# Attention and mixture of experts on one core: two output tiles and one memory tile for the attention's results, scatters to disjoint views, the 64-row block second

## The chip, the cores and the metric

The kernel runs on one core of one Trainium2 chip. The time is the device time of one execution in microseconds. The kernel before took 972.42 us (median of three runs, 971.52 to 975.38). The engines are named as in the profile: PE multiplies matrices, DVE and ACT are the vector and the scalar engine, POOL is the general one, SP issues transfers. PSUM is the memory that PE writes, in eight banks of 128 x 512 float32.

## The reference

For 8 batches and 8 heads, with 576 rows of 64 columns, the kernel computes a causal softmax attention and a retrieval from a memory, mixes both by a gate per head, and sends the 4608 rows of 512 through a mixture of 8 experts, each of which takes exactly 576 rows, chosen greedily from the largest logit down.

```python
scores = np.where(causal, -1e9, scale * q @ k.T)
a = exp(scores - max); a /= a.sum(-1) + 1e-09
local = a @ v
q_p = phi(q)                       # x+1 if x > 0, else exp(x)
mem_out = (q_p @ M_prev) / (q_p @ z_prev + 1e-06)
x = g * mem_out + (1 - g) * local  # 4608 x 512
logits = x @ w_gate                # 4608 x 8
for idx in np.argsort(-logits.flatten()):
    tok, e = idx // E, idx % E     # taken if tok is free and e has room (576)
out[mask_e] = np.maximum(x[mask_e] @ w1[e], 0.0) @ w2[e]
```

## The kernel before

*Attention.* The work is cut into 16 units, one batch and four heads each. For a unit, q, k and v are loaded, split into two float16 parts each, and transposed by PE. For a head, PE computes the scores into the buffers `pb`; DVE takes the row maxima (L1197); ACT takes exponentials to float16 (`ph`, L1334), and the rest that float16 leaves out goes to `pl`: ACT writes the exponential again in float32, in PSUM (L1338) or in SBUF (L1341), and then DVE (L1339, called P2v) or POOL (L1342, called P2) subtracts `ph`. A string `p2k` of twelve letters says for each block of a unit which of the two it is.

`outs` (L1351) makes a head's result. The memory part AVm takes ten matmuls (`avs<-mh,pT`), the attention part AV1, AV2 and AV3 45 matmuls of 65 columns. All go into one PSUM tile `avs` of three banks. There are two head buffers in it: buffer b has slots 0 to 6 in bank 2b and slots 7 to 9 in a part of the middle bank 1. Slots 0 to 4 take the attention, 5 to 9 the memory, and column 64 of a slot has the denominator. Then DVE works: N0 (L1385 and L1386) takes the ten denominators, N1 (L1390) inverts them, N2 (L1389, `xt<-avs`) scales the memory part into `xt`, N2b (L1389, `avs<-avs`) scales the attention part in place, and N3 (L1403) adds the two. In one head of four, N2 scales all ten slots and POOL adds (L1397). After that come a cast, a subtraction, transposes and the logits of the rows.

*Order.* A list scheduler, run when the kernel is built, puts all instructions in one order from costs given with each node (`SC.add('AVm',[('T',300)],...)`: 300 ns on PE), from limited buffers (`av`=2 head buffers) and from two tables of numbers, PR for the attention and PM for the experts: due times, offsets and biases that choose an engine where several can do a node. An engine runs its instructions in that order. The waits between engines are put in by the tile framework from the tiles that instructions read and write.

*Routing and experts* (`moe_all`, L1537). For each expert a threshold is found in 12 rounds (DVE L1774, ACT L1772, PE, DVE L1780 and L1781). The 576 rows that pass are listed: DVE counts (L1612) and computes row numbers `idx` (L1614), and POOL fetches the rows by five indirect transfers (L1617). Weights come as float32 and are split into `wh` and `wl` by ACT (L1688, L1689) and POOL (L1690); for the first pieces of expert 0 by ACT (L1685) and DVE (L1686). PE multiplies by the first matrix (`ph`, `prem`), ACT and DVE take the relu in two parts (L1732, L1733), PE multiplies by the second (`py`) in row blocks of 128, 128, 128, 128 and 64. A block of 128 is copied by ACT to `ys` (L1747); the block of 64 is put together by ACT (L1749) and DVE (L1750). POOL writes each block to its rows by an indirect transfer (L1752), and `chain('scat')` makes each of the 40 wait for the one before. Routing of expert n+1 runs beside the matmuls of expert n.

Of the kernel before, what the change touches and what calls it, by code (L numbers as in the profile page):

```python
# [23 lines left out]
          'kba': -30628.42,  # L24
          'kbd': -21514.39,
          'kbv': -30457.33,
          'kha': -9689.05,
          'khp': 68039.52,
          'khv': 14252.18,
          'klp': -32138.21,  # L30
          'klv': -19015.13,
          'mh2a': 18046.34,
          'mh2v': -7557.72,
          'mha': -6556.62,
          'mhv': 118047.29,
          'mlp': -61301.72,
          'mlv': 103205.55,
          'mra': 13094.26,
          'mrv': -49929.19,
          'mza': 13667.92,  # L40
          'mzv': 154718.09,
          'nap': -923.34,
          'nav': -3267.9,
          'nca': -17356.34,
          'ncp': 19952.5,
          'ncv': -19147.84,
          'nsp': -33806.3,
          'nsv': 8700.47,
          'p2p': 3448.83,
          'p2v': -5.41,  # L50
          'p4sp': -99613.75,
          'p4sv': -14317.61,
          'pha': -24715.3,
          'php': 10489.25,
          'phra': -10695.76,
          'phrv': 20287.52,
          'phv': -24278.1,
          'plp': 4297.99,
          'plv': 4879.76,
          'prepca': -46562.05,  # L60
          'prepcv': -134550.89,
          'qha': -51241.95,
          'qhp': 17974.64,
          'qhv': -60171.16,
          'qlp': 26287.18,
          'qlv': 78420.0,
          'qmovea': 42586.74,
          'qmoved': 5914.55,
          'qmovev': -9885.0,
          'tea': -3123.88,  # L70
          'tev': -3783.25,
          'vha': -3050.15,
          'vhp': 15722.78,
          'vhv': 48350.7,
          'vlp': 27996.84,
          'vlv': 29979.61,
          'xtea': -62406.89,
          'xtev': 142184.48},
 'dl': {'0': {'AV': 3.03,
              'MX': -439.58,  # L80
              'N': -45.87,
              'P2': 95.25,
              'S': -79.48,
              'fin1': 396.93,
              'fin2': 87.35,
              'kb': 3.48,
              'kh': -937.23,
              'kl': -795.9,
              'kt': 387.88,
              'lk': -688.72,  # L90
              'lm': -210.42,
              'lq': -541.06,
              'lv': -99.14,
              'maxrem': -157.75,
              'mfin': 328.48,
              'mfin2': -56.76,
              'mfin3': -180.29,
              'mh': -838.83,
              'ml': 193.21,
              'mz': -1034.64,  # L100
              'nadd': -286.28,
              'ncast': 852.81,
              'nsub': -703.35,
              'ph': -141.8,
              'phe': -764.62,
              'phr': -38.36,
              'phs': 62.7,
              'pl': -977.2,
              'prep': 200.37,
              'proc24': 671.37,  # L110
              'pt': 192.37,
              'qh': -404.47,
              'ql': 386.07,
              'qmove': 129.64,
              'qt': -168.61,
              'sj4': -1434.02,
              'vh': 667.29,
              'vl': 490.09},
        '1': {'AV': 58.78,
              'MX': -104.28,  # L120
              'N': -347.1,
              'P2': -339.06,
              'S': 606.52,
              'fin1': 484.59,
              'fin2': 2.45,
              'kb': 126.23,
              'kh': -563.06,
              'kl': 507.8,
              'kt': 591.73,
              'lk': -540.92,  # L130
              'lm': -577.58,
              'lq': -166.76,
              'lv': -66.59,
              'maxrem': 342.62,
              'mfin': -545.34,
              'mfin2': 9.06,
              'mfin3': -80.01,
              'mh': -618.46,
              'ml': 449.29,
              'mz': 14.48,  # L140
              'nadd': -926.32,
              'ncast': -198.57,
              'nsub': 506.43,
              'ph': -560.71,
              'phe': -372.41,
              'phr': -876.37,
              'phs': 209.62,
              'pl': 213.14,
              'prep': 164.36,
              'proc24': 454.72,  # L150
              'pt': 233.41,
              'qh': -427.92,
              'ql': 1274.93,
              'qmove': 1075.02,
              'qt': 47.11,
              'sj4': -45.54,
              'vh': -285.68,
              'vl': -176.11},
        '10': {'AV': 758.58,
               'MX': -73.66,  # L160
               'N': 72.38,
               'P2': 279.63,
               'S': -8.46,
               'fin1': -248.92,
               'fin2': 347.06,
               'kb': 358.91,
               'kh': 442.41,
               'kl': 79.29,
               'kt': -298.24,
               'lk': -767.97,  # L170
               'lm': 14.63,
               'lq': -633.6,
               'lv': 673.6,
               'maxrem': 724.62,
               'mfin': -318.66,
               'mfin2': 386.87,
               'mfin3': 137.35,
               'mh': 981.75,
               'ml': -129.7,
               'mz': 550.95,  # L180
               'nadd': -120.05,
               'ncast': 1.51,
               'nsub': -229.44,
               'ph': 489.25,
               'phe': 997.89,
               'phr': -1284.21,
               'phs': 165.79,
               'pl': -224.45,
               'prep': 191.53,
               'proc24': -144.35,  # L190
               'pt': -242.79,
               'qh': 501.96,
               'ql': 984.38,
               'qmove': -284.76,
               'qt': -711.9,
               'sj4': -187.91,
               'vh': 1156.16,
               'vl': -17.9},
        '11': {'AV': 355.99,
               'MX': -108.14,  # L200
               'N': -177.3,
               'P2': -1118.12,
               'S': 356.14,
               'fin1': 358.76,
               'fin2': 223.29,
               'kb': -146.64,
               'kh': -152.48,
               'kl': 559.23,
               'kt': -15.25,
               'lk': 955.17,  # L210
               'lm': 246.97,
               'lq': 882.81,
               'lv': -420.65,
               'maxrem': 30.53,
               'mfin': -41.22,
               'mfin2': 83.89,
               'mfin3': -400.44,
               'mh': -51.28,
               'ml': -126.76,
               'mz': -129.3,  # L220
               'nadd': 107.08,
               'ncast': -1366.45,
               'nsub': 536.08,
               'ph': -283.95,
               'phe': -649.23,
               'phr': -270.74,
               'phs': -481.4,
               'pl': 292.58,
               'prep': -518.41,
               'proc24': -4.05,  # L230
               'pt': -249.01,
               'qh': 480.34,
               'ql': 615.5,
               'qmove': 459.89,
               'qt': -26.77,
               'sj4': 164.57,
               'vh': -414.34,
               'vl': 21.65},
        '12': {'AV': 167.39,
               'MX': 1.03,  # L240
               'N': 559.11,
               'P2': -154.37,
               'S': -49.69,
               'fin1': 221.57,
               'fin2': 527.79,
               'kb': 1200.71,
               'kh': -74.53,
               'kl': -144.63,
               'kt': -309.14,
               'lk': -221.84,  # L250
               'lm': -263.39,
               'lq': -614.17,
               'lv': 244.4,
               'maxrem': 565.59,
               'mfin': 257.23,
               'mfin2': 16.16,
               'mfin3': 507.27,
               'mh': 215.36,
               'ml': 291.75,
               'mz': 463.51,  # L260
               'nadd': -356.78,
               'ncast': 12.76,
               'nsub': 868.62,
# [631 lines left out]
class Sched:  # L895
# [18 lines left out]
    def run(self,tol=100,sem=170,same=110,t0=0.0,hwg=450,dlat=1300,dend=950,ph=2800.0,thr=3060,pel=60):  # L914
# [20 lines left out]
        def pick(e):  # L935
            C=cand[e]; best=None; L=[]; Q=line[e]
            f=free[e]
            for c in C:
# [7 lines left out]
                elif e=='V' and (x.slack or x.nm in LK) and s<poolb-1: s=poolb-1  # L946
# [11 lines left out]
        while left:  # L958
            b=None
# [931 lines left out]
```

## Time and profile before

| | |
|---|---|
| median of three runs | 972.42 us (971.52 to 975.38) |
| profiled execution | 974.23 us, span 972.40 us |
| PE, PEld busy | 814.7 us (84%), 523.4 us |
| DVE, ACT, POOL busy | 717.4 us (74%), 578.3 us, 599.7 us (62%) |
| attention | 0 to about 500 us |
| first expert's threshold and list | about 500 to 560 us |
| experts' matmuls | about 560 to 962.5 us |
| mean granted clock of PE | 0.947 |

The span is from the first to the last instruction of the profiled execution; its time as a run is 1.83 us longer. Busy shares of the whole span are means over these stages. A wait in the profile is idle time of an engine, put down to the instruction whose end came last; the chain of waits is followed back from the last instruction.

### The profile page before, as it was taken

Reading aid. Unit: us, or ns where it says so; the run is one execution under the profiler, and the core shown is the slowest. Engines: PE = TensorE matmul, PEld = TensorE weight load, DVE = VectorE, ACT = ScalarE, POOL = GpSimd, SP = SyncE. Lnnn points to the kernel's source line nnn. Section 1 sums busy time; section 2 is a strip of 40 time slices with the busy share of each in tenths; the row PEclk is TensorE's granted clock in tenths of the full one; section 3 lists DMA queues with packets and bytes.
Section 4 is the critical chain, followed back from the end, with each engine's and each line's share of the span. In section 5 each row is a group of like instructions: output and inputs, shape, how many; then the busy total and the mean of one; then the engine's idle time right before and its main releaser. Section 6 shows DMA issues by size and latency. Waiting matters only on the chain.

```text
span 972.4 us, 25309 instructions
## 1 busy us (share of the span) xinstructions
PE 814.7 (84%) x9736; PEld 523.4 (54%) x9736; DVE 717.4 (74%) x2385; ACT 578.3 (59%) x1046; POOL 599.7 (62%) x594
## 2 busy tenths in 40 slices
PE   4587888878888888888831797999999999999995
PEld 3365666656667666767620543445454444444442
DVE  8998889998889899896678977768787777502010
ACT  4475776677587767768622557483838383754110
POOL 7768787889889878968610237382647373585101
PEclk9897999999899999999955699899999999999999
DMA  5566454528555443533411427362737273692101
GB/s 130 117 142 147 111 118 93 128 66 168 115 131 124 92 105 69 118 66 66 94 36 61 162 79 220 127 177 81 231 102 237 94 232 102 216 269 78 38 12 38
DMA packets 230302, 116.49 MB, mean 120 GB/s; under 512 B 199013, under 2 KB 208229, under 8 KB 230181
## 3 DMA queue, kind: packets, MB, share of 16 engines
q1 hardware_dynamic: 224293, 96.00, 39.1%
q0 software_dynamic: 5888, 18.88, 5.8%
q8 instruction: 76, 1.25, 0.5%
q14 instruction: 45, 0.37, 0.1%
HBM read 72.40 MB, written 18.87 MB: 94 GB/s over the span
## 4 chain that ended last, share of the span: by engine, by line
PE 44%; DVE 7%; issue 1%; ACT 1%; DMA 1%; POOL 0%; POOLq 0%; DVEq 0%; ACTq 0%
PE py L1540 19%; PE ph L1540 16%; PE avs L1041 3%; PE prem L1540 2%; DVE scr L1774 2%; PE pr L1540 1%; DMA out_dram<-ys,idx 1%; PE pb L1041 1%; DVE xt L1389 1%; PE pl L1540 1%; DVE avs L1389 1%; DVE xt L1403 0%; DVE th L1781 0%; ACT wh L1689 0%; DVE kk L1780 0%
## 5 line engine op out<-in xcount | busy, mean ns | idle before, releaser
L1690 POOL TENSOR_TENSOR wl<-wst,wh 128x1024 f16<-128x1024 f32 x60 | 127.6, 2150 | 81.9 <-ACT wh L1689 64.7
L1540 PE MATMUL ph<-xT,wh 128*128 128x512 f16 (+1 forms) x560 | 164.0, 368 | 1.7 <-DVE hl L1733 1.0
L1334 ACT ACTIVATE ph<-pb 128x512 f16<-128x512 f32 x192 | 115.7, 602 | 42.5 <-PE pb L1041 32.0
L1197 DVE TENSOR_REDUCE mx<-pb 128x1 f32<-128x512 f32 (+3 forms) x256 | 123.3, 547 | 2.2 <-PE pb L1041 2.0
L1041 PE MATMUL avs<-V,ph 128*128 128x65 f16 x1792 | 103.6, 194 | 24.8 <-DVE xt L1389 11.4
L1752 POOL DMA_INDIRECT out_dram<-ys,idx x40 | 38.7, 968 | 126.3 <-ACT ys L1747 70.9
L1041 PEld LDWEIGHTS <-ph 128*128 128x128 f16 x1792 | 94.3, 99 | 33.4 <-issue 30.3
L1342 POOL TENSOR_TENSOR pl<-pf,ph 128x512 f16<-128x512 f32 x80 | 95.2, 1193 | 19.7 <-ACT pf L1341 18.3
L1041 PE MATMUL pb<-qT,kT 128*128 128x64 f16 (+3 forms) x576 | 102.3, 242 | 6.0 <-DVE mx L1197 2.8
L1540 PEld LDWEIGHTS <-wh 128*128 128x128 f16 x1072 | 68.7, 99 | 59.3 <-issue 3.8
L1041 PE MATMUL avs<-V,pl 128*128 128x65 f16 x896 | 99.5, 197 | 0.0
L1540 PE MATMUL ph<-xT,wl 128*128 128x512 f16 (+1 forms) x280 | 98.8, 367 | 0.0
L1041 PE MATMUL pb<-kT,qM 128*128 128x256 f16 (+5 forms) x384 | 83.9, 314 | 16.9 <-DVE mx L1197 9.4
L1041 PE MATMUL pb<-qM,kB 128*128 128x64 f16 (+3 forms) x576 | 97.1, 241 | 0.1
L1540 PE MATMUL py<-wl,hh 128*128 128x512 f16 x256 | 97.0, 379 | 0.0
L1540 PE MATMUL py<-wh,hh 128*128 128x512 f16 x256 | 97.0, 379 | 0.0
L1540 PE MATMUL prem<-xT,wh 128*128 128x64 f16 x512 | 96.7, 193 | 0.0
L1733 DVE SCALAR_TENSOR_TENSOR hl<-ph,hh 128x512 f16<-128x512 f32 x64 | 44.0, 688 | 65.2 <-ACT hh L1732 64.6
L1774 DVE TENSOR_SCALAR_CACHE_REDUCE scr<-p_LwT,th 128x320 f16<-128x320 f32 x168 | 85.1, 544 | 2.7
L1772 ACT ACTIVATE scs<-p_LwT,th 128x320 f16<-128x320 f32 x84 | 47.0, 560 | 64.8 <-DVE th L1781 50.7
L1041 PEld LDWEIGHTS <-pl 128*128 128x128 f16 x896 | 85.2, 99 | 0.0
L1732 ACT ACTIVATE hh<-ph 128x512 f16<-128x512 f32 x64 | 37.9, 594 | 74.9 <-PE ph L1540 49.6
(289 smaller groups left out, 2293.1 us busy)
## 6 DMA issues: line engine op xcount, KB each, us to landing
wst<-in_moe_w_dram SPq DMA_DIRECT2D x32, 1024.0 KB
kf<-in_k_dram SPq DMA_DIRECT2D x64, 128.0 KB
qf<-in_q_dram SPq DMA_DIRECT2D x64, 128.0 KB
vf<-in_v_dram SPq DMA_DIRECT2D x64, 128.0 KB
xd<-xs SPq DMA_DIRECT2D x16, 512.0 KB
kB<-kT SPq DMA_DIRECT2D x15, 288.0 KB
kf<-in_k_dram SPq DMA_DIRECT2D x32, 32.0 KB
qf<-in_q_dram SPq DMA_DIRECT2D x32, 32.0 KB
```

The costliest lines, as they stand in the source:

```text
L1041: def MM(*a,**kw): mm(*a,skip_group_check=True,**kw)
L1197: R=lambda o,i: nc.vector.tensor_reduce(o,i,axis=mybir.AxisListType.X,op=ALU.max)
L1334: c=SC.add('Eh',[('A',478)],lambda x,a=a: nc.scalar.activation(phs_[x.buf['ph']][:,0:512],pbb[a.buf['pb']],AF.Exp,scale=0.125),acq=('ph',) ...
L1342: e=SC.add('P2',[('P',1113)],lambda x,c=c,d=d: nc.gpsimd.tensor_sub(pls_[c.buf['ph']][:,0:512],pfs[d.buf['pf']],phs_[c.buf['ph']][:,0:512] ...
L1389: MU=lambda o,i,d: nc.vector.tensor_tensor(o,i,d,op=ALU.mult)
L1540: def MM(*a,**kw): mm(*a,skip_group_check=True,**kw)
L1690: SC.add('sp',[('P',2079)],lambda x,ws=ws,k=k,s=s: G_.tensor_sub(wl[:,k,s],ws(),wh[:,k,s]),r=[key+('h',)],w=[key+('l',)],after=[b],rel=rel ...
L1732: b=SC.add('hh',[('A',478)],lambda x,a0=a0,f=f: A_.activation(hh[:,f],phb[a0.buf['ph']],AF.Relu),w=[('hh',f)],after=[y],prio=pr('hh',n,pos ...
L1733: SC.add('hl',[('V',602)],lambda x,a0=a0,f=f: V_.scalar_tensor_tensor(hl[:,f],phb[a0.buf['ph']],0.0,hh[:,f],op0=ALU.max,op1=ALU.subtract), ...
L1752: z=SC.add('scat',[('P',655 if i<4 else 330,'p',0,(1034,'n'))],lambda x,e=e,i=i,r_=r_: G_.indirect_dma_start(out=out,out_offset=bass.Indir ...
L1772: SC.add('sign',[('A',547)],lambda x,j=j,t_=t_,c_=c_: A_.activation(scs[j-KV],LwT,AF.Sign,bias=t_[:,4:5],accum_out=c_[:,j:j+1]),r=['LwT',( ...
L1774: V(462,lambda x,j=j,t_=t_,c_=c_: V_.tensor_scalar(scr[j],LwT,t_[:,j+1:j+2],0.0,op0=ALU.is_ge,op1=ALU.add,accum_out=c_[:,j:j+1]),r=['LwT', ...
```

## The change

1. `avs` is replaced by three tiles of one bank: `avo0` and `avo1` (slots 0 to 4, the attention part, pool `av` of 2) and `avm` (the memory part, pool `am` of 1). AVm comes behind AV3 of its head. N2 is one operation and gives `avm` free, N3 gives `avo` free. N0 waits for AV3 and AVm.
2. The gate's weights (L1152) and most of the routing's constants (L1498 to L1506) are computed by POOL instead of DVE.
3. The scatters write through disjoint views of the output, without the chain. The row blocks of the second matrix come in the order 0, 4, 1, 2, 3 (block 4 has 64 rows). `idx` is computed by one operation from PSUM instead of two. Of expert 0's weights, two pieces instead of four are split by ACT and DVE (`s0` from 4 to 2).
4. Costs of gathers and scatters in the scheduler and nearly all numbers of both tables are others; `p2k` is `vpvpvvvvpvpv` instead of `vpvpvvpvpvpv`, that is one P2 more on DVE in each unit.

```diff
-    a0=SC.add('AVm',[('T',300)],...,acq=('av',),after=ch('A'),prio=pr('AV',u,3*j))
-    a1=SC.add('AV1',[('T',279)],...,after=[a0]+ce,prio=pr('AV',u,3*j+.1))
+    a1=SC.add('AV1',[('T',279)],...,acq=('av',),after=ch('A')+ce,prio=pr('AV',u,3*j+.1))
     ...
+    a0=SC.add('AVm',[('T',300)],...,acq=('am',),after=ch('Am')+[a3],prio=pr('AV',u,3*j+.4))
-    own=lambda a,b: avs[:,2*bi(),65*a:65*b]...
-    mid=lambda: avs[:,1,195*bi():195*bi()+195]...
+    own=lambda a,b: avo[a1.buf['av']][:,65*a:65*b]...
+    mem=lambda: avm[:,0:325]...
-    n0=SC.add('N0',[('V',158)],f,...,after=[a3],...)
+    n0=SC.add('N0',[('V',158)],f,...,after=[a3,a0],...)
-    def f(x): t=...; MU(t[:,0:2],own(5,7)...,dv(5,7)); MU(t[:,2:5],mid()...,dv(7,10))
+    def f(x): MU(xts[x.buf['xt']][:,0],mem()[:,:,0:64],dv(5,10))
     ...
-        nc.vector.tensor_scalar(wf,wf,64.0,...); nc.vector.tensor_copy(...); nc.vector.tensor_sub(...)
+        nc.gpsimd.tensor_scalar(wf,wf,64.0,...); nc.gpsimd.tensor_copy(...); nc.gpsimd.tensor_sub(...)
     ...
+    outv=dram_disjoint_views(out,40)
-    V_.tensor_scalar(tks[:,a:b],e[:,a:b,1],-64.0,...); V_.tensor_tensor(idx[:,a:b],tks[:,a:b],pps[:,a:b],op=ALU.add)
+    V_.scalar_tensor_tensor(idx[:,a:b],e[:,a:b,1],-64.0,pps[:,a:b],op0=ALU.mult,op1=ALU.add)
-        for i in range(5):
+        for i in (0,4,1,2,3):
-    z=SC.add('scat',[('P',655 if i<4 else 330,...)],... out=out,...,after=[e]+chain('scat'),...)
+    SC.add('scat',[('P',1250 if i<4 else 1200,...)],... out=outv[5*n+i],...,after=[e],...)
```

On DVE, in the second half of the attention, this is one head's N0 to N3 before; `avs` is the tile of three banks, `de` the denominators, `pl` the residuals of P2v, and the waits behind a row are the engines that it waits for.

```order
685 L1390 RECIPROCAL de_159<-de_159 128x10 [waits DVE_49]
686 L1389 TENSOR_TENSOR xt_161<-avs,de_159 128x128 [waits DVE_49]
687 L1389 TENSOR_TENSOR xt_161<-avs,de_159 128x192
688 L1271 SCALAR_TENSOR_TENSOR ef_110<-qf_106,pb_176 128x512 [waits Activation_49]
689 L1389 TENSOR_TENSOR avs<-avs,de_159 128x5x64 [waits DVE_49,PE_49]
690 L1339 TENSOR_TENSOR pl_143<-pb_173,ph_135 128x512 [waits Activation_49]
691 L1403 TENSOR_TENSOR xt_161<-avs,xt_161 128x320 [waits DVE_49,PE_49]
```

The same of a head after the change (N0 is L1304 and L1305 there, N2 and N2b L1308, N3 L1322, P2v L1261):

```order
586 L1304 SCALAR_TENSOR_TENSOR de_161<-avo_103,eps 128x5 [waits PE_49]
587 L1305 SCALAR_TENSOR_TENSOR de_161<-avm,eps 128x5 [waits PE_49]
588 L1261 TENSOR_TENSOR pl_143<-pb_177,ph_135 128x512 [waits Activation_49]
589 L1309 RECIPROCAL de_161<-de_161 128x10 [waits DVE_49]
590 L1308 TENSOR_TENSOR xt_164<-avm,de_161 128x320 [waits DVE_49,Pool_49]
591 L1308 TENSOR_TENSOR avo_103<-avo_103,de_161 128x5x64
592 L1006 COPY qT_122<-pb_177 128x1024 [waits PE_49]
593 L1322 TENSOR_TENSOR xt_164<-avo_103,xt_164 128x320 [waits DVE_49]
```

N2 is one operation on `avm`, and the waits for PE stand at N0 alone: N2b and N3 have none.

On POOL, the last scatters before; `DMASW` are the transfers issued by POOL itself.

```order
577 L1752 DMA out_dram<-ys_9855,idx_9837 4608x512 [waits DMASW2_49,Activation_49]
578 L1752 DMA out_dram<-ys_9853,idx_9837 4608x512 [waits DMASW3_49,Activation_49]
579 L1752 DMA out_dram<-ys_9854,idx_9837 4608x512 [waits DMASW4_49,Activation_49]
580 L1752 DMA out_dram<-ys_9855,idx_9837 4608x512 [waits DMASW5_49,Activation_49]
581 L1752 DMA out_dram<-ys_9853,idx_9837 4608x512 [waits DMASW6_49,DVE_49]
```

The last five after the change:

```order
578 L1675 DMA out_dram<-ys_9807,idx_9790 4608x512 [waits DMASW3_49,Activation_49]
579 L1675 DMA out_dram<-ys_9806,idx_9790 4608x512 [waits DMASW4_49,DVE_49]
580 L1675 DMA out_dram<-ys_9807,idx_9790 4608x512 [waits DMASW5_49,Activation_49]
581 L1675 DMA out_dram<-ys_9808,idx_9790 4608x512 [waits DMASW6_49,Activation_49]
582 L1675 DMA out_dram<-ys_9806,idx_9790 4608x512 [waits DMASW7_49,Activation_49]
```

The scatter behind DVE's sum (64 rows) has moved from the last place to the second of five. Before, the transfer that a scatter waits for is the scatter just ahead of it; after, it is the one eight ahead, whose semaphore it uses again.

## Rows read from the trace of the kernel before

**Rows 1.** The table by stage: the stretch in us, its length, and the busy time (and number) of PE, PEld, DVE, ACT and POOL, then PE's granted clock, the DMA share and GB/s.

```profile
40.00:100.00 60.00, 47.84 (x698) 36.10 (x697) 54.41 (x128) 38.25 (x70) 46.69 (x42) 0.91 0.66 148
100.00:430.00 330.00, 275.47 (x4962) 220.99 (x4959) 294.16 (x785) 241.00 (x448) 271.45 (x288) 0.98 0.50 109
430.00:500.00 70.00, 53.64 (x1116) 45.34 (x1112) 49.71 (x158) 45.31 (x93) 46.53 (x52) 0.93 0.33 69
500.00:540.00 40.00, 7.29 (x40) 3.92 (x40) 33.55 (x183) 11.95 (x30) 3.08 (x3) 0.50 0.24 90
...
560.00:960.00 400.00, 393.38 (x2573) 189.33 (x2570) 231.55 (x974) 213.47 (x357) 197.89 (x133) 0.99 0.44 141
```

**Rows 2.** What DVE waited for from 40 to 500 us: in all, times, the longest (us).

```profile
DVE avs L1389 <- PE avs L1041: 14.9, 19, 1.8
DVE de L1385 <- PE avs L1041: 10.0, 17, 1.3
DVE xt L1389 <- PE avs L1041: 9.4, 18, 1.8
DVE xt L1403 <- PE avs L1041: 7.6, 13, 0.9
```

**Rows 3.** What PE waited for in the same stretch.

```profile
PE avs L1041 <- DVE xt L1389: 17.3, 30, 1.9
...
PE avs L1041 <- DVE avs L1389: 9.4, 15, 1.8
PE avs L1041 <- DVE xt L1403: 9.0, 15, 2.3
```

**Rows 4.** The chain of waits, at 442 to 448 us and at the first round of the first threshold: start and length in us, engine, what.

```profile
442.91 0.82 PE avs L1041 x21
...
443.76 0.50 DVE xt L1403
...
444.30 0.94 PE avs L1041 x25
...
447.00 1.10 PE avs L1041 x30
...
503.76 0.94 DVE scr L1774 x4
```

**Rows 5.** Groups of instructions of the whole span, shapes apart: line, engine, operation, out<-in, count, then busy us, mean ns of one, idle time before and what ended it.

```profile
L1339 DVE TENSOR_TENSOR pl<-pb,ph 128x512 f16<-128x512 f32 x112 | 76.0, 681 | 4.4 <-ACT pb L1338 3.6 <-issue 0.6
L1342 POOL TENSOR_TENSOR pl<-pf,ph 128x512 f16<-128x512 f32 x80 | 95.2, 1193 | 19.7 <-ACT pf L1341 18.3 <-DMA qf<-in_q_dram 1.2
L1389 DVE TENSOR_TENSOR avs<-avs,de 128x320 f32<-128x320 f32 x48 | 23.8, 496 | 15.5 <-PE avs L1041 14.9
L1403 DVE TENSOR_TENSOR xt<-avs,xt 128x320 f32<-128x320 f32 x48 | 23.4, 487 | 8.5 <-PE avs L1041 7.6
L1389 DVE TENSOR_TENSOR xt<-avs,de 128x192 f32<-128x192 f32 x64 | 22.2, 348 | 0.0
L1084 DVE COPY kT<-pb 128x1024 f16<-128x1024 f16 x29 | 19.5, 681 | 0.6 <-PE pb L1183 0.4
L1389 DVE TENSOR_TENSOR xt<-avs,de 128x128 f32<-128x128 f32 x48 | 13.9, 289 | 8.4 <-PE avs L1041 6.5 <-POOL h L1174 0.6
L1390 DVE RECIPROCAL de<-de 128x10 f32<-128x10 f32 x64 | 13.2, 209 | 0.7
L1389 DVE TENSOR_TENSOR xt<-avs,de 128x448 f32<-128x448 f32 x16 | 10.0, 622 | 3.2 <-PE avs L1041 2.9
L1174 DVE TENSOR_TENSOR p<-ef,p 128x640 f16<-128x640 f32 x2 | 2.9, 1450 | 0.0
```

**Rows 6.** The operations that go to POOL: the busy time of DVE on L1152 alone from 29 to 36 us; DVE's last of them and POOL's run beside it by time; the first and the last of the ten constants (line, duration in ns, start).

```profile
29.00:36.00 7.00, 5.44 (x3) 0.75 0.54 121
...
32.22 3.16 DVE L1152 TENSOR_TENSOR wgs<-wf,wgs 128x32 f16<-128x32 f32 x1
...
32.75 2.58 POOL L1286 TENSOR_TENSOR V<-vf,V 128x512 f16<-128x512 f32 x2
...
L1498 DVE CAST EW<-it x1: 884/884/884, 130.5 to 130.5; 128x8 f32<-128x8 int32 x1
...
L1506 DVE CAST sio<-i x1: 833/833/833, 182.3 to 182.3; 40x640 f16<-40x640 int32 x1
```

**Rows 7.** By time, the split on DVE and the fifth gather of expert 0 on POOL.

```profile
543.34 1.23 DVE L1686 SCALAR_TENSOR_TENSOR wl<-wst,wh 128x1024 f16<-128x1024 f32 x1
...
545.91 0.92 POOL L1617 DMA_INDIRECT xg<-xd,idx  x1 [2.24 <-DVE idx L1614]
```

**Rows 8.** What POOL and ACT waited for at earlier scatters.

```profile
POOL out_dram L1752 <- DMA out_dram<-ys,idx: 17.1, 7, 3.8
...
ACT ys L1747 <- DMA out_dram<-ys,idx: 1.7, 1, 1.7
```

**Rows 9.** The end, by time, on ACT, POOL, DVE and PE.

```profile
959.14 0.60 ACT L1747 ACTIVATE ys<-py 128x512 f32<-128x512 f32 x1 [4.63 <-PE py L1540]
962.54 0.59 ACT L1749 ACTIVATE y<-py 64x512 f32<-64x512 f32 x1 [2.81 <-PE py L1540]
...
960.01 0.96 POOL L1752 DMA_INDIRECT out_dram<-ys,idx  x1 [4.27 <-ACT ys L1747]
964.13 0.90 POOL L1752 DMA_INDIRECT out_dram<-ys,idx  x1 [3.16 <-DVE ys L1750]
...
963.17 0.68 DVE L1750 SCALAR_TENSOR_TENSOR ys<-py,y 64x512 f32<-64x512 f32 x1 [22.91 <-ACT y L1749]
...
962.12 0.38 PE L1540 MATMUL py<-wl,hr 128*128 128x512 f16 x1
```

More of the change, by code (lines that the diff above doesn't have):

```diff
@@ L5 @@
 import concourse.tile as tile
+from concourse.ap import dram_disjoint_views
 from concourse import mybir
@@ L41 @@
-          'mzv': 154718.09,
+          'kba': -38256.38,
+          'kbd': -26666.66,
+          'kbv': -40060.57,
+          'kha': 14508.09,
+          'khp': 79231.15,
+          'khv': 24617.63,
+          'klp': -1086.28,
+          'klv': 16564.27,
+          'mh2a': 20115.95,
+          'mh2v': -71452.4,
+          'mha': 22820.34,
+          'mhv': 89368.52,
+          'mlp': -31325.33,
+          'mlv': 98087.6,
+          'mra': 17856.1,
+          'mrv': -40742.45,
+          'mza': 48409.13,
@@ new lines @@
+          'p4sp': -101839.76,
+          'p4sv': 7041.96,
+          'pha': -31945.75,
+          'php': 29271.45,
+          'phra': -17422.93,
+          'phrv': 21464.53,
+          'phv': -15662.98,
+          'plp': -19639.54,
+          'plv': 43456.26,
+          'prepca': -6518.9,
+          'prepcv': -117462.96,
+          'qha': -48927.36,
+          'qhp': 53729.35,
+          'qhv': -70868.4,
+          'qlp': 66042.22,
+          'qlv': 67290.35,
+          'qmovea': 37764.26,
+          'qmoved': 9935.43,
@@ L780 @@
          'phr': 'v',
-         'pl': 'p*v',
-         'prepc': 'v',
+         'pl': '***',
+         'prepc': 'a',
          'qh': 'p',
-         'ql': 'p*p',
-         'qmove': 'aaad',
-         'te': 'v*vvv*av*a**',
+         'ql': 'ppv',
+         'qmove': 'a*d*',
+         'te': '**v*vva**avv',
          'vh': 'p',
-         'vl': 'ppv',
-         'xte': 'a*av'},
- 'run': {'tol': 19.5},
+         'vl': 'p*p',
+         'xte': '***v'},
+ 'run': {'tol': 13.3},
  'strict': 1,
@@ L945, in pick @@
                     if s<lockV and c[1][-1].__class__ is not tuple: s=lockV
-                elif e=='V' and (x.slack or x.nm in LK) and s<poolb-1: s=poolb-1
+                elif e=='V' and (x.slack or x.nm in LK) and s<poolb+1: s=poolb+1
                 if len(x.alts)>1:
@@ L951, in pick @@
                     for a in x.alts:
-                        if a is not c[1] and max(free[a[0]],t,poolb-1 if a[0]=='V' and x.nm in LK else 0)+bi(a)<mine: worse=True; break
+                        if a is not c[1] and max(free[a[0]],t,poolb+1 if a[0]=='V' and x.nm in LK else 0)+bi(a)<mine: worse=True; break
                     if worse: continue
@@ L1036, in attention @@
     V16=[sb.tile([128,20,132],F16,name=f'V16{i}') for i in range(2)]
-    avs=ps.tile([128,3,512],F32,name='avs')
+    avo=[ps.tile([128,512],F32,name=f'avo{i}') for i in range(2)]; avm=ps.tile([128,512],F32,name='avm')
     P_=PR
@@ L1631, in lists @@
             V(516,lambda x: cnt((3,4)),r=['pl','nr'],w=['pp2'],k=2)
[L1632 removed]
+            V(74,lambda x: ids(0,5),r=['ple','pp','pp2'],w=allx)
             for i in range(5): gather(i)
@@ L1751, in ffn @@
             chain('ys',e)
[L1752 removed]
+            SC.add('scat',[('P',1250 if i<4 else 1200,'p',0,(1250,'n'))],lambda x,e=e,i=i,r_=r_: G_.indirect_dma_start(out=outv[5*n+i],out_offset=bass.IndirectOffsetOnAxis(ap=idx[0:r_,i:i+1],axis=0),in_=yss[e.buf['ys']][0:r_],in_offset=None),r=[('idx',n%3,i)],after=[e],rel=[('ys',e)],prio=pr('scat',n,pos[0]))
     for n in range(8):
```

1609 lines of the change are left out of this document (745 added, 864 removed).

## The prediction

> **What bounds the kernel now.** The page's busy shares, with PE the fullest engine and DVE the next, are means over stages with different limits, so I read the table by stage first [rows 1]. The reader is to see three regimes. From 100 to 430 us, the middle of the attention, DVE is the fullest engine (294.16 of 330 us, 89%), PE has 275.47 and POOL 271.45. From 500 to 560 us the first expert is routed, a chain of 12 rounds of small operations in which PE is mostly idle (7.29 of the first 40 us). From 560 to 960 us PE has 393.38 of 400 us: this stage is bound by its matmuls, and nothing on another engine can shorten it unless it ends a wait of PE.
>
> Second, the waits. In the attention from 40 to 500 us DVE is busy for 54.41 + 294.16 + 49.71 = 398.3 of 460 us, so 61.7 us are idle. Four rows of the DVE waits name PE's writes of `avs` as what ended them: 14.9, 10.0, 9.4 and 7.6 us [rows 2]. PE in its turn waits for DVE's reads of the same tile: 17.3, 9.4 and 9.0 us, three long rows [rows 3]. Third, the chain of waits shows how both can be true [rows 4]: DVE scales a head's memory part (L1389 `xt`), PE runs 21 matmuls into `avs`, only then DVE adds (L1403), only then PE runs 25 more, and so on; two engines that each have other work pass one tile to and fro. In the order of the instructions, N2b and N3 of one head stand with a wait for PE although the matmuls of their own head had to end before N0: what they wait for is the other head's matmuls, in another bank of the tile. So the tile is followed as a whole, and most of these waits are not for data.
>
> **The change part by part.**
>
> *The attention tiles.* With `avo0`, `avo1` and `avm` no two heads share a tile except `avm`, which is passed on in full from head to head. The three rows that end on N2, N2b and N3 (14.9 + 9.4 + 7.6 = 31.9 us) are then without a cause; the 10.0 us of L1385 (N0) wait for the head's own matmuls and stay. Bounds: all 31.9 us come off, or none, since the matmuls whose end DVE awaited still have to run and DVE may meet the same lateness one step further on, at N0, which now also waits for the memory matmuls at the end of its own head. I take half, -16: in the chain the waits come in pairs, one of DVE and one of PE, and the matmuls between (0.82 to 1.10 us [rows 4]) are as long as the waits, so one engine of the two can run on and the other fills the gap only if it has something ready.
>
> *A new wait.* `avm` is single. A head's memory matmuls must wait until DVE has read the head before (N2); 36 heads have that wait as an instruction on PE. Behind it in PE's queue stand the scores and transposes of the next unit, for which ACT and DVE wait. Its price is not in the trace; the nearest row is PE's wait for `xt` L1389, 17.3 us in 30 waits, 0.58 us each [rows 3]. Upper bound 36 x 0.58 = 20.8 us, lower bound nothing, since N2 now comes early (the N2b that stood in its way in both directions is free). I take +3: PE has room in this stage (47.84 + 275.47 + 53.64 = 377.0 of 460 us busy), so most of it passes unseen.
>
> *DVE's work.* The in-line heads' N2 becomes one 128x320 operation instead of 128x128 + 128x192. Before, 48 x 289 + 64 x 348 + 16 x 622 ns = 13.9 + 22.2 + 10.0 = 46.1 us [rows 5]; after, 80 operations of 128x320 at about 0.49 us (the rows L1389 `avs` 496 ns and L1403 487 ns), 39.2 us: -6.9. The table of residuals gives DVE one more P2 per unit, 16 x 681 ns = +10.9 [rows 5], and takes 16 x 1193 ns = 19.1 us from POOL. Retuned choices take some copies, casts and subtractions of 128x1024, 128x640 and 128x256 from DVE: two copies `kT` (2 x 681 ns), one like it, two subtractions `p<-ef` (2 x 1450 ns) and two smaller ones, some 6 us [rows 5]. The gate's weights (L1152, three operations, 5.44 us) and the routing's constants (ten operations of 0.15 to 1.3 us, L1498 to L1506, the first of 884 and the last of 833 ns, 5.9 us in all) go to POOL [rows 6]. Together -6.9 + 10.9 - 6 - 11.3 = -13.3 us of DVE time in the attention. On the path stands what falls where DVE is the last: bounds 0 and -13.3, and I take half, -7, since even in its fullest stage DVE is waiting a tenth of the time. POOL's bill is lighter by more than it gains, so it is no new bound.
>
> The moved constants have a catch in the trace. The subtraction of 128x32 takes 3158 ns from 32.22 us and ends at 35.38 us; POOL's run of two subtractions begins at 32.75 and ends at 35.33 us [rows 6]. An operation on so few columns lasted until POOL was done. The Trainium skill, "SBUF — State Buffer", section "SBUF: two separate sides", says that VectorE with two SBUF inputs and GpSimd take one port pair as an exclusive lock, held for a whole instruction. The trace agrees: 3.16 us for 32 columns. By that rule the move works in both directions: about 13 new operations of POOL can hold up those of DVE that read SBUF twice. By the rows alone the constants are worth -11.3 of DVE's time; by the rule, if each new operation blocked DVE for some 0.3 us, an estimate by that page, 4 us would come back, which lies inside the bounds above. P2 on DVE reads one input from PSUM, so it should keep its 681 ns.
>
> *The first expert's list.* The row numbers come in one operation instead of two, and only two instead of four weight pieces are split by DVE. In the trace the fifth gather starts at 545.91 us, POOL idle for 2.24 us before it, and the DVE split of 1.23 us at 543.34 stands just ahead of the count that it needs [rows 7]. In the new order all five row numbers come ahead of the splits. Between nothing and -2.2; I take -1.3, that split.
>
> *The scatters.* They no longer wait for one another. POOL waited 17.1 us for earlier scatters in 7 places [rows 8], but PE's stage of experts is full, so they matter only where they reach PE. Once ACT's copy of a result waited 1.7 us for a scatter to free its buffer, and the activations of the next matmuls stand behind it on ACT [rows 8]: bounds 0 and -1.7, I take -1. The gathers of the next expert, in the same queue, can only come earlier.
>
> *The end.* The 64-row block now comes second, so the last block is one of 128 rows with the single copy of ACT. Before: the last matmul starts at 962.12 and ends at 962.50, ACT's copy 962.54 to 963.13, DVE's sum 963.17 to 963.85, POOL's issue 964.13 to 965.03, and the span ends at 972.40 [rows 9]. After: copy 0.60, gap 0.27 (959.74 to 960.01 in the block before), issue: 0.68 + 0.04 us of DVE go, -0.7. Twice the rows in the last transfer could take that back: bounds -0.7 and +0.7; I take -0.7, since the scatter of 128 rows before it was not longer on POOL (0.96 against 0.90 us).
>
> **Sum.** -16 + 3 - 7 - 1.3 - 1 - 0.7 = -23.0 us. The profiled execution took 974.23 us (span 972.40 and 1.83 around it), so 951.2 us; it lies 1.8 us above the median of the runs, 972.42. The forecast is 950 us. With every best end the sum is -31.9 - 13.3 - 2.2 - 1.7 - 0.7 = -49.8 (923 us by the median); with every worst end it is +20.8 + 0.7 = +21.5 (994 us).
>
> **The rivals.**
>
> *The waits only move.* N0 waits for ten matmuls more at the end of its head and PE still sets when a head's results are there: the 10.0 us row of L1385 grows by what the others lose. For it: DVE and PE are close in load (294.16 against 275.47 us), and POOL with 271.45 is close behind. Against it: the same matmuls had to be done before, only earlier. Then a quarter of the 31.9 us and of the 13.3 us stay gained, 11.3, with the last three terms 14.3, less the 3 of the new wait: 11.3 us, 961 us.
>
> *All of it counts.* DVE reaches 95% of the stage. Then 31.9 + 10 + 3 = 45 us come off, 927 us; for it speaks the length of the pairs in the chain, against it that POOL and PE also have 82 to 83% here and would have to feed DVE faster.
>
> *Slower: the single memory tile.* The loop over `avm` is ten matmuls, N0, reciprocal, N2: about 0.4 + 0.25 + 0.21 + 0.49 us and four hand-overs of 0.04, some 1.5 us, into which DVE's list puts one or two other operations of about 0.6 us [rows 4, 5]. Half of the memory groups have 83 matmuls or fewer between them and the group before in PE's list, 3.1 us at 0.94 us for 25. If in these 32 heads PE then stands still for 1.5 us, that is 48 us, more than the 31.9 us that go; with -7 and -3 it gives 48 - 31.9 - 10 = +6 us, 978 us. It decides from the point where the mean wait at `avm` passes 1.3 us in these 32 heads. Against it speaks that PE has 83 us of slack and that the order puts other matmuls between.
>
> *The change does not do what it says.* If the tiles were still guarded together only the last three terms would go, 3.0 us, since DVE's own gain of 13.3 us would be idle time: about 969 us. The order of the changed kernel shows N2b without a wait for PE, so I give it little.
>
> **How the numbers follow.** The forecast, 940 to 960 us, has 0.50; waits only moved, 960 to 967.5, 0.17; all of it, under 940, 0.15; no change, 0.10; the slower one 0.08. A measurement of this kernel can tell about 0.5% from no change, 4.9 us. So faster 0.82, same 0.10, slower 0.08. The range leaves out the upper tenth and the lower tenth: 932 to 968 us.
>
> **What would show it.** In the new profile: the rows of DVE at N2, N2b and N3 that end on PE should be under 8 us together; PE's three rows on `avs` from DVE should shrink to one on `avm`; DVE's share from 100 us to the attention's end should pass 91%. The first round of the threshold (L1774), at 503.76 us before [rows 4], should start near 484. The fifth gather should follow the others without a hole, PE's stretch from first to last expert should keep its length to 2 us, and the span should end about 9.2 us after the last matmul instead of 9.9. I am wrong if DVE's idle time from 40 us on stays over 50 us, or if PE's waits for N2 at `avm` pass 30 us; and if the time falls while the DVE waits stay, then the shorter DVE list was the cause, not the tiles.

## The result, and the profile after

The changed kernel took 934.08 us (median of four runs, 930.70 to 937.75) against 972.72 us; the ratio is 0.960, 95% interval 0.955 to 0.965. The forecast was 950 us in a range of 932 to 968. In a later session, in six more runs, it took 924.29 us (921.67 to 927.62), ratio 0.949 (0.945 to 0.952); how the two differ is taken up below. In the first session the direction and the range held; in the later one the time lies 8 us below the lower end of the range. The gain of 38.6 us, and 50 in the later session, was well above the 22 us forecast.

The table by stage of the changed kernel (columns as in [rows 1]) and the waits of DVE and of PE in the attention:

```profile
40.00:456.00 416.00, 365.09 (x6757) 296.25 (x6757) 386.86 (x1014) 323.72 (x611) 345.91 (x377) 0.97 0.54 118
...
100.00:400.00 300.00, 266.55 (x4928) 215.60 (x4926) 285.21 (x746) 236.28 (x443) 261.23 (x289) 0.98 0.55 120
...
515.00:917.00 402.00, 394.15 (x2574) 189.33 (x2573) 221.56 (x955) 210.80 (x352) 196.78 (x134) 1.00 0.48 140
```

```profile
DVE pl L1261 <- ACT pb L1260: 9.2, 17, 1.6
...
DVE de L1305 <- PE avm L963: 1.6, 5, 0.5
...
DVE de L1304 <- PE avo L963: 0.7, 2, 0.4
...
PE avo L963 <- POOL pl L1264: 1.4, 1, 1.4
PE avo L963 <- DVE xt L1322: 1.3, 1, 1.3
```

DVE is idle for 29.1 us from 40 us to the end of the attention (456 us), 61.7 before; its share in the middle is 95.1%, 89% before. The four rows of [rows 2] with their 41.9 us have shrunk to 2.3 us at N0. Of PE's three rows on DVE's reads [rows 3], 35.7 us, 1.3 us are left, and no row of PE's waits names `avm`. The first round of the first threshold shows where the gain lies (the second number of a row is the first start):

```profile
L1697 DVE TENSOR_SCALAR_CACHE_REDUCE scr<-p_LwT,th x168: 530/544/548, 458.5 to 759.2; 128x320 f16<-128x320 f32 x168
```

It starts at 458.5 us instead of 503.76 [rows 4]: 45.2 us come from the attention. From there to the last matmul it took 461.5 us in this profile, 458.7 before, so in this one profile 2.7 us were lost among the experts. The end is as forecast; the last matmul's run, then ACT's copy, then POOL's issue:

```profile
918.08 1.89 PE L1461 MATMUL py<-wh,hl 128*128 128x512 f16 x8
...
920.01 0.60 ACT L1670 ACTIVATE ys<-py 128x512 f32<-128x512 f32 x1 [4.58 <-PE py L1461]
...
920.88 0.96 POOL L1675 DMA_INDIRECT out_dram<-ys,idx  x1 [4.22 <-ACT ys L1670]
```

The span ends at 929.30, 9.33 us after 919.97; before it was 9.90 us.

### The profile page after: what moved, and what is told of

Same layout as the page of the kernel before. It is cut to its first block, busy times and chain, and to the rows that moved or that the text cites. A ratio compares the mean times of both kernels' runs of the same rounds, so it can differ in the third digit from the quotient of the medians.

```text
span 929.3 us, 25223 instructions
## 1 busy us (share of the span) xinstructions
PE 804.9 (87%) x9736; PEld 517.6 (56%) x9736; DVE 693.6 (75%) x2319; ACT 579.3 (62%) x1053; POOL 589.6 (63%) x595
## 4 chain that ended last, share of the span: by engine, by line
PE 49%; DVE 20%; issue 12%; ACT 7%; POOL 5%; DMA 5%; SPq 1%; POOLq 0%; DVEq 0%; ACTq 0%
PE py L1461 15%; PE ph L1461 15%; PE pb L963 8%; DVE mx L1119 6%; PE avo L963 4%; PE pb L1105 2%; DVE scr L1697 2%; DVE pl L1261 2%; PE prem L1461 2%; DMA xT<-xs 2%; ACT ph L1256 2%; ACT pb L1260 1%; PE pr L1461 1%; PE avm L963 1%; POOL out_dram L1675 1%
## 5 line engine op out<-in xcount | busy, mean ns | idle before, releaser
L1613 POOL TENSOR_TENSOR wl<-wst,wh 128x1024 f16<-128x1024 f32 x62 | 131.4, 2141 | 83.8 <-ACT wh L1612 76.2
L963 PE MATMUL avo<-V,ph 128*128 128x65 f16 x1792 | 102.3, 194 | 1.5 <-DVE xt L1322 1.3
L963 PE MATMUL avo<-V,pl 128*128 128x65 f16 x896 | 98.1, 197 | 1.4 <-POOL pl L1264 1.4
L1261 DVE TENSOR_TENSOR pl<-pb,ph 128x512 f16<-128x512 f32 x128 | 86.4, 678 | 9.9 <-ACT pb L1260 9.2
L1264 POOL TENSOR_TENSOR pl<-pf,ph 128x512 f16<-128x512 f32 x64 | 75.4, 1178 | 22.8 <-ACT pf L1263 22.8
```

Source lines behind the costliest of these rows:

```text
L963: def MM(*a,**kw): mm(*a,skip_group_check=True,**kw)
L1261: e=SC.add('P2v',[('V',602)],lambda x,a=a,c=c: nc.vector.tensor_sub(pls_[c.buf['ph']][:,0:512],pbb[a.buf['pb']],phs_[c.buf['ph']][:,0:512] ...
L1264: e=SC.add('P2',[('P',1113)],lambda x,c=c,d=d: nc.gpsimd.tensor_sub(pls_[c.buf['ph']][:,0:512],pfs[d.buf['pf']],phs_[c.buf['ph']][:,0:512] ...
L1613: SC.add('sp',[('P',2079)],lambda x,ws=ws,k=k,s=s: G_.tensor_sub(wl[:,k,s],ws(),wh[:,k,s]),r=[key+('h',)],w=[key+('l',)],after=[b],rel=rel ...
```

## The experiments

The theory: one tile of three banks made DVE and PE wait for work on the other head's bank, and the split removes it. The rivals: DVE's shorter list; the new order; the experts. Times are medians, ratios are to runs of the kernel before in the same session; the first round, in each profile, is the first start of the threshold's first operation.

**One tile again, order as changed.**

```diff
-    avo=[ps.tile([128,512],F32,name=f'avo{i}') for i in range(2)]; avm=ps.tile([128,512],F32,name='avm')
+    avs=ps.tile([128,3,512],F32,name='avs'); avo=[avs[:,0],avs[:,2]]; avm=avs[:,1]
```

> The changed kernel with one edit: the three result tiles are slices of one tile of three banks again; every engine's order is the same as in the changed kernel, and 69 of DVE's N2, N2b and N3 have a wait for PE again (none in the changed kernel). If the tiles are the cause of the gain, the time goes back by about the 32 us of such waits that the trace of before shows, to 960 to 970 us, and DVE's rows on PE at N2, N2b and N3 are over 20 us together. If the shorter list of DVE or the new order is the cause, it stays within 5 us of the changed kernel's 934.

Measured: 963.28 us, ratio 0.990 (0.987 to 0.993). The waits of DVE are back:

```profile
DVE de L1304 <- PE avs L963: 14.2, 25, 1.7
DVE avs L1308 <- PE avs L963: 9.6, 16, 1.1
DVE xt L1322 <- PE avs L963: 7.6, 11, 1.9
...
DVE xt L1308 <- PE avs L963: 5.6, 13, 0.7
```

At N2, N2b and N3 they are 22.8 us together, and the first round starts at 500.1 us. Without the split the whole rest of the change is worth 1%. The forecast of 960 to 970 us held, and the rival that the shorter list or the new order alone carries the gain is out.

**The split alone, order as before.**

```diff
-    avs=ps.tile([128,3,512],F32,name='avs')
+    avs=[ps.tile([128,512],F32,name=f'avs{i}') for i in range(3)]
-    return avs[:,2*b,65*i:65*i+65] if i<7 else avs[:,1,65*(3*b+i-7):65*(3*b+i-6)]
+    return avs[2*b][:,65*i:65*i+65] if i<7 else avs[1][:,65*(3*b+i-7):65*(3*b+i-6)]
     ...
```

> The kernel before with one edit: its three banks are three tiles, two of one head buffer each and the middle one shared by both; the order of every engine is unchanged, and the instructions at L1389 and L1403 with a wait for PE fall from 74 to 16. If the tiles alone carry the gain, the time falls to 940 to 955 us, with no instruction moved. If the waits only move to N0 or to other engines as long as the order is the old one, it stays over 965 us.

Measured: 936.98 us, ratio 0.965 (0.960 to 0.969), 3 us below the lower end that the theory gave. Waits of DVE, and the first round:

```profile
DVE de L1385 <- PE avs L1041: 4.4, 9, 1.0
...
DVE de L1386 <- PE avs L1041: 0.9, 2, 0.5
...
DVE xt L1389 <- PE avs L1041: 0.7, 3, 0.3
...
L1774 DVE TENSOR_SCALAR_CACHE_REDUCE scr<-p_LwT,th x168: 527/543/548, 469.2 to 780.0; 128x320 f16<-128x320 f32 x168
```

Not one instruction moved on any engine. The first round comes 34.5 us earlier, and the waits of [rows 2] fall from 41.9 to 6.0 us. They hardly moved on: of DVE's other rows the one that grew most, the maxima (L1197) on PE, went from 2.0 to 6.3 us. N0, which waits for its own head's matmuls, halved too; I take it that PE was late with those because it had itself been waiting.

The traces show the cause itself. In the kernel before, none of the 352 operations of DVE on `avs` overlaps in time with a matmul of PE into it; with the split, 154 of the 352 do. By the Trainium skill, "PSUM — Partial Sum Buffer", section "PSUM bank collisions raise a hardware error", two engines are to be guarded from one another by bank and partition quadrant, in the simple version by bank. This run agrees: with one tile to a bank the waits are 36 us shorter.

**Attention and experts apart.** Two kernels join the attention of one with the table and code of the experts of the other.

> The attention of the changed kernel with the routing and the experts of the kernel before (its table, its block order, the chain of scatters, two operations for the row numbers, four pieces split by ACT and DVE). The traces put 45.2 us of the gain ahead of the first round of the threshold, and the part behind it is 2.1 us longer than before. If that holds, this kernel is about 2 us faster than the changed one, 930 to 933 us. If the forecast's terms for the experts hold (-1.3, -1, -0.7 us), it is 3 us slower than the changed one, 937 us.

> The reverse: the attention of the kernel before with the routing and the experts of the changed one. By the traces' milestones it takes 2 us more than before, 974 to 976 us; by the forecast's three terms 3 us less, 969 to 970 us.

Measured: the changed attention with the old experts 929.80 us, ratio 0.956 (0.954 to 0.959); the old attention with the new experts 967.10 us, ratio 0.994 (0.992 to 0.996). So the new experts gain 6 us with the old attention, which neither expectation had: the stage from the first round to the last matmul took 452.7 us. With the old experts it took 458.7 us in the kernel before, 455.8 with the split alone and 456.9 with the changed attention, so 3 to 6 us are gained there. In the new attention they had seemed to lose, in the one profile at hand.

**The changed kernel again, no edit.**

> The changed kernel once more, with no edit. In its first profile DVE stood still three times at L1703 for 2.5 to 3.6 us while the matmul that it names had ended, PE then waited, and the experts' stage was 9 us longer (461.5 us from the first round of the threshold to the last matmul) than in the two other kernels with the same experts (452.5 and 452.7 us). If these stalls belong to this kernel, they stand at the same rounds again and the time is 931 to 938 us. If they are accidents of an execution, the stage is 453 us in this profile and some runs fall to 922 to 926 us.

Measured: 924.29 us, ratio 0.949 (0.945 to 0.952), and the stage took 452.0 us. The stalls of the first profile are not there. This is what one of them looked like (kernel as changed, first profile; DVE and PE by time, then the table by stage):

```profile
735.10 0.16 DVE L1703 SCALAR_TENSOR_TENSOR kk<-pr,need 128x3 f32<-128x3 f32 x1 [3.60 <-PE prem L1461]
...
731.51 0.17 PE L1461 MATMUL pr<-c,blk 128*128 128x3 f16 x1
...
736.64 0.18 PE L1461 MATMUL pr<-c,blk 128*128 128x3 f16 x1 [2.97 <-DVE scr L1697]
...
731.00:737.00 6.00, 3.03 (x27) 1.54 (x26) 2.33 (x10) 3.11 (x7) 5.37 (x5) 1.00 0.81 203
737.00:743.00 6.00, 6.00 (x39) 2.75 (x37) 4.01 (x18) 3.58 (x9) 3.19 (x2) 0.72 0.91 165
```

The matmul (`pr`) that `kk` needs ended at 731.68; `kk` started at 735.10, and DVE did nothing from 731.50 on. PE ran out of work that did not need the next round and stood for 2.97 us, and in the 6 us behind it the granted clock was 0.72, a mix of its levels of 2.4 and 1.2 GHz. There were three such stalls (2.47, 3.28 and 3.60 us) in that profile, none in four later profiles with the same order of the experts behind this attention. The profile of the kernel before has one too, where the matmul had ended at 599.43 us (PE, then DVE):

```profile
599.26 0.17 PE L1540 MATMUL pr<-c,blk 128*128 128x3 f16 x1
...
601.26 0.16 DVE L1780 SCALAR_TENSOR_TENSOR kk<-pr,need 128x3 f32<-128x3 f32 x1 [2.46 <-PE py L1540]
```

So its 458.7 us hold a stall as well, and the stalls are not of the changed kernel alone. The first session's four runs were all 930 us or more and the later one's six all under 928, which points to the session; only one of those four runs was profiled. All four stalls stand while the rows of POOL's five gathers come in (from 729.6 to 735.8 us for the one shown first), but the later profiles have these gathers without a stall. What held DVE is open.

**N2 in two operations.**

```diff
-    def f(x): MU(xts[x.buf['xt']][:,0],mem()[:,:,0:64],dv(5,10))
+    def f(x): t=xts[x.buf['xt']][:,0]; MU(t[:,0:2],mem()[:,0:2,0:64],dv(5,7)); MU(t[:,2:5],mem()[:,2:5,0:64],dv(7,10))
```

> The changed kernel with one edit: N2 of the in-line heads is two operations on avm again, of 128 and 192 columns, so DVE has 48 x (289 + 348 - 484 ns) = 7.3 us more, at the place in its order where it was; nothing else moves. If the attention is bound by DVE from end to end, as the rival that takes all of DVE's work says, the time rises by 7 us. By the forecast's half it rises by 3.7 us. If DVE's list has become slack without the waits, it stays within 2 us.

Measured: 925.86 us, ratio 0.951 (0.948 to 0.954). The groups of this kernel show the added work, 48 x (347 + 287) ns in place of 48 x 484:

```profile
L1308 DVE TENSOR_TENSOR xt<-avm,de 128x192 f32<-128x192 f32 x48 | 16.7, 347 | 0.0
L1308 DVE TENSOR_TENSOR xt<-avm,de 128x128 f32<-128x128 f32 x48 | 13.8, 287 | 1.7
...
40.00:456.00 416.00, 365.45 (x6755) 296.64 (x6752) 388.86 (x1055) 324.01 (x611) 346.36 (x376) 0.97 0.54 117
```

By durations DVE got 7.2 us more, but its busy time from 40 to 456 us rose by 2.0 us only (388.86 against 386.86); two such operations overlap in part. The time rose by 1.6 us, and the intervals overlap. A rise of 7 us is excluded. But since the edit gave DVE 2 us and not 7, it does not decide whether DVE bounds the attention from end to end.

**Constants on DVE again, at the same places.**

```diff
-    nc.gpsimd.tensor_scalar(wf,wf,64.0,...); nc.gpsimd.tensor_copy(...); nc.gpsimd.tensor_sub(...)
+    nc.vector.tensor_scalar(wf,wf,64.0,...); nc.vector.tensor_copy(...); nc.vector.tensor_sub(...)
     ...
```

> The changed kernel with one edit: the gate's weights and the routing's constants are computed by DVE again, at the places in the program where POOL has them; the order of every engine is otherwise the same. DVE has about 11.3 us more by the trace of before. By the forecast's half the time rises by 5.7 us; if DVE is the bound from end to end, by 11; if the short operations on DVE lasted only because POOL held them up and find other places now, by 2 to 4 us.

Measured: 927.53 us, ratio 0.953 (0.950 to 0.957): 3 us, with intervals that overlap. The gate's subtraction there, and POOL by time:

```profile
L1074 DVE TENSOR_TENSOR wgs<-wf,wgs x1: 1024/1024/1024, 29.8 to 29.8; 128x32 f16<-128x32 f32 x1
...
28.14 2.59 POOL L1208 TENSOR_TENSOR V<-vf,V 128x768 f16<-128x768 f32 x2
```

It took 1.02 us at this place and 3.16 us in the kernel before [rows 6]; on POOL, in the changed kernel, 0.25 us. Again it ended with POOL's run: at 30.8 us, and POOL's two subtractions at 30.73. So its length on DVE was not its own work, and the price of 11.3 us read from the rows of before was not a price that DVE pays at every place: here the same 13 operations last 5.9 us together. By the Trainium skill, "SBUF — State Buffer", section "SBUF: two separate sides", an operation of VectorE with two SBUF inputs and one of GpSimd that reads SBUF share a port pair as an exclusive lock, and the one that starts first has it for its whole instruction. This trace agrees: DVE's subtraction ended 0.1 us behind the one of POOL that ran when it started. In the kernel before it lasted through two subtractions of POOL that started after it [rows 6], which the rule alone does not give.

**Scatters wait for one another again** (the one edit: `out=out` for `out=outv[5*n+i]`).

> The changed kernel with one edit: the scatters write to the whole output again, so that each waits for the one before; no instruction moves. By the forecast's term (-1) the time rises by 1 us, at most 2, since PE's stage of experts is full. If the waits at the scatters hold back the next expert's gathers on POOL, behind them in its order, the time rises by 5 us or more.

Measured: 925.33 us, ratio 0.949 (0.946 to 0.953), 1.0 us above the changed kernel and not to be told from it. As forecast, these waits cost next to nothing.

**The attention's old table on the new layout.**

```diff
-PR = {'bias': ..., 'p2k': 'vpvpvvvvpvpv', 'run': {'tol': 13.3}, ...}
+PR = {'bias': ..., 'p2k': 'vpvpvvpvpvpv', 'run': {'tol': 19.5}, ...}
```

> The changed kernel with the attention's table of the kernel before (biases, due times, pins, and p2k, so 16 residuals fewer on DVE and 16 more on POOL); the three tiles, AVm behind AV3, the constants on POOL and the experts stay as changed. With split tiles alone and everything else old, the first round of the threshold came at 469.2 us; in the changed kernel at 458.5 to 461.5. If the tiles' new layout (no bank shared between heads) gives that rest, the first round stays near 460 us and the time within 3 us of the changed kernel's 924. If the retuned table gives it, the first round is near 470 us and the time near 934.

Measured: 946.80 us, ratio 0.974 (0.972 to 0.977): slower than both expectations, and than the split with everything old. PE's waits in its attention, and the first round:

```profile
PE pb L963 <- DVE pl L1261: 12.7, 15, 3.7
PE pb L963 <- DVE mx L1119: 11.8, 32, 2.5
PE pb L1171 <- DVE mx L1168: 8.3, 5, 4.0
...
L1697 DVE TENSOR_SCALAR_CACHE_REDUCE scr<-p_LwT,th x168: 532/544/548, 480.5 to 772.6; 128x320 f16<-128x320 f32 x168
```

The new layout with the old table reaches the first round at 480.5 us, the old layout split at 469.2, the new one with its own table at 458.5 to 461.5. The memory part behind AV3 is no gain by itself: on the new layout the new table is worth some 20 us against the old one.

**The experts' old table; four pieces split by ACT and DVE; the blocks in the old order.** Three kernels, each the changed one with one edit (the table PM of before; `s0` 4; `for i in range(5)`), and in all three the scheduler makes a new order of the experts from it.

> The changed kernel with the experts' table of the kernel before; block order, disjoint scatters, row numbers in one operation stay as changed (the number of pieces split by ACT and DVE goes back to four with the table). The new experts were worth 6 us with the old attention, by their stage 452.7 instead of 458.8 us; the gain stood at the change from expert 0 to expert 1. If the order by the table is its cause, the time rises by 4 to 6 us, to 928 to 931. If block order, scatters and row numbers are, it stays within 2 us of 924.

> The changed kernel with four of expert 0's weight pieces split by ACT and DVE, as before, instead of two; the scheduler orders the experts anew from it. In the old experts expert 0's hidden part ended 74 us after the first round of the threshold, in the new ones 80. If the two pieces that wait for three operations each are the cause, the time falls by 2 to 5 us and this is faster than both kernels. If the routing of expert 1, which the new order puts beside expert 0, is the cause, it stays within 2 us or is slower.

> The changed kernel with the row blocks of the second matrix in the old order 0 to 4; the scheduler orders the experts anew from it. The tail from the last matmul to the end was 9.90 to 9.97 us with the 64-row block last and 9.24 to 9.33 with it second, so 0.65 us more are sure. If that is all that the block order does, the time rises by under 2 us. If it is also what shortened the change from expert 0 to expert 1 (the experts' table and the scatters' waits did not), the stage from the first round of the threshold to the last matmul goes from 452 to 456 us or more and the time rises by 5 us.

Measured: 924.09 us with the old table, ratio 0.951 (0.948 to 0.954); 926.22 us with four pieces, 0.953 (0.951 to 0.956); 927.43 us with the old block order, 0.953 (0.951 to 0.955). Against the 924.29 us of the changed kernel, itself of another session, the table gives nothing that can be told, and four pieces no gain, as the second of their two expectations had it. The block order may give about 3 us, though the intervals overlap: 0.7 at the end (9.99 us behind the last matmul against 9.29) and 2.0 in the stage (454.0 against 452.0 us). The rest of the experts' 6 us stands where expert 0 passes to expert 1. The relu of the 64-row block marks it, here in the old attention with the new experts:

```profile
586.89 0.69 DVE L1659 SCALAR_TENSOR_TENSOR hr<-prem,hr 128x512 f16<-128x512 f32 x1
...
635.18 0.68 DVE L1659 SCALAR_TENSOR_TENSOR hr<-prem,hr 128x512 f16<-128x512 f32 x1
```

From expert 0 to expert 1 that is 48.3 us, against 60.2 us in the kernel before (578.04 to 638.23 us); expert 0 itself is 6.8 us later after the first round, so 5 us are gained. From the first round to the relu of expert 1 the three profiles with the old experts took 132.8 to 134.5 us, the changed kernel in the later session 128.4. With the table, the scatters, the block order or the two pieces undone singly it is 128.4 to 130.3 us, so none of them alone is the cause. The row numbers in one operation and the planner's new costs of gathers and scatters are left; they were not tried, and this stays open.

## Why the prediction was right, point by point

*The attention tiles, -16.* The mechanism was right and the size was the mis-sized term: the split alone gave -34.5 us in the attention and 36 us of time. The step that failed is "I take half", with its reason that one engine can run on while the other waits. In the chain of [rows 4] both engines' waits came from each other's. I read the 41.9 us of DVE and 35.7 us of PE as one loss seen twice: with the split alone DVE's rows lost 35.9 us, PE's three rows fell to 8.0, and the time fell by 36 us, about either sum and not both. "The 10.0 us of L1385 stay" failed as well: with the split alone N0 waits for 5.3 us (4.4 at L1385) and in the changed kernel for 2.3 us, and no wait moved to N0.

*The new wait at the single `avm`, +3.* Nothing: no row of PE names it. The slower rival had its cause there and is ruled out.

*DVE's work, -7.* Not shown by the runs that touched it: putting N2's second operation back cost 1.6 us, the constants 3.2, neither beyond its interval, and the first round came at 460.3 and 459.7 us, as in the unedited kernel. Two prices were too high: the 13 moved operations last 5.9 us at another place and not 11.3, and N2's second operation, put back, adds 2.0 us of busy time where its durations say 7.2. Yet the changed attention reaches the first round 8 to 11 us before the split in the old order. From 40 us to the first round (before, split alone, changed, changed with the old table; the third time is DVE's):

```profile
40.00:503.70 463.70, 377.88 (x6770) 302.90 (x6768) 400.39 (x1087) 324.57 (x610) 365.62 (x383) 0.96 0.49 107
40.00:469.20 429.20, 371.68 (x6772) 301.77 (x6770) 396.12 (x1087) 322.75 (x610) 364.65 (x383) 0.95 0.54 116
40.00:458.50 418.50, 365.90 (x6760) 296.62 (x6758) 388.53 (x1031) 323.98 (x613) 346.68 (x377) 0.96 0.54 117
40.00:480.50 440.50, 368.77 (x6754) 298.88 (x6752) 387.89 (x1019) 321.06 (x606) 363.19 (x389) 0.96 0.52 112
```

The split alone takes 30.2 us of DVE's idle time (63.3 to 33.1). From there to the changed kernel DVE is busy for 7.6 us less and idle for 3.1 us less. But with the old table it is as little busy and idle for 52.6 us: the same amount of DVE's work takes 22 us longer. So the order that the table makes matters, and the forecast had priced it at nothing; how much of the 8 to 11 us is the order's and how much the shorter list's is not shown.

*The first expert's list, -1.3.* The fifth gather started 39.65 us after the first round instead of 42.15, 2.5 us earlier, a little beyond the bound; but expert 0's relu came later after the first round (80.1 us against 74.3; 76.3 with four pieces again), and with four pieces the time was no better.

*The scatters, -1, and the end, -0.7.* The scatters gave 1.0 us by the run that put the waits back, inside its noise; the end gave 0.57 to 0.70 us by the profiles.

*What was to be seen.* The rows at N2, N2b and N3 under 8 us (none is left that ends on PE), DVE's share over 91% (95.1%) and the end at 9.2 us (9.33) came as told; the first round came at 458.5, not near 484. "PE's stretch should keep its length to 2 us" failed: from the first round to the last matmul it was 2.7 us longer in the first profile, and 452.0 us in the later session against 455.8 to 458.7 with the old experts. Of the rivals "all of it counts", given 0.15 at 927 us, came nearest, but the experts' 6 us are not in it.

*What was luck.* The 934.08 us lie inside the range because the first session's runs were some 10 us slower; the profiled one of them lost about that in the experts' stage (461.5 against 452.0 us). In the later session, whose profile has no such stall, the time is 924.29 us and misses the range on its lower side: half of the tiles' gain had been taken off, and no term had the gain where expert 0 passes to expert 1.

## What to carry to other kernels

Look at which tile a wait is for, not only at the engine: if an instruction waits for a matmul into a bank that it does not touch, the tile is too large, and splitting it costs no instruction. When two engines wait for each other over one such tile, the two sums can be one loss: here all of the smaller one came back (36 of 35.7 us), not half. A table tuned for one layout is part of that layout: with the other layout's table this one lost 20 us, so a change of layout and a retuned order are to be measured both together and crossed.

## What was not expected of the hardware

DVE stood still for 2.5 to 3.6 us at an instruction whose matmul had long ended, three times in one execution, once in the kernel before, and in none of four later profiles with the changed kernel's order; PE's granted clock then fell to 0.72 over the 6 us behind a gap of 2.97 us. An operation on 32 columns took 3.16, 1.02 or 0.25 us by its place and engine, so the duration of a short operation in a trace is not its cost elsewhere.
